# A hand-ordered attention and gating block: tile 0 in halves, first queries by token halves, new orders

## The chip, the core and the metric

The kernel runs on one core of a Trainium2 chip. The metric is the device time of one execution, in microseconds. The engines are named as in the profile: PE (TensorE), DVE (VectorE), ACT (ScalarE), POOL (GpSimd) and SP (SyncE, which only issues DMAs here). PEld is PE's loading of weights.

## What is computed

```python
h  = x + A(layernorm(x), wqkv, wo)
h2 = h + B(layernorm(h), w_in, w_sp, b_sp, w_out)

# A: linear attention, 32 heads of 16
q, k, v = split(x @ wqkv)
phi = lambda t: where(t > 0, t + 1, exp(t)) + 1e-6
kv, z = einsum(phi(k), v), sum(phi(k))
o = (phi(q) @ kv) / (phi(q) . z + 1e-6)
A = o @ wo

# B: gated mixing
z  = gelu(x @ w_in);  z1, z2 = first half, layernorm(second half)
g  = w_sp @ z2 + b_sp          # mixes tokens
B  = (z1 * g) @ w_out
```

x has 2048 tokens of 512, all data are bf16; w_in has 1792 columns, w_sp is 2048 x 2048.

## The kernel before

The 2048 tokens are 16 tiles of 128, and four groups of four tiles. The stages are these.

1. Tile n of x is loaded (`load`, L495), its statistics are made on DVE (L576, L580), the factor from the variance on ACT for tiles 0 to 3 (L590 Ln, L592 Exp) and on POOL for the pairs above (L595, L597), and DVE normalises it into `xn1` (L611, in the profile pk_xn_z). It is transposed into `xT`: tiles 0 to 3 on PE (L645), with a copy out of PSUM on ACT (L652); the others by a DMA transpose that SP issues (L637).
2. Keys of a pair of tiles (`kv_proj`, L734) and queries of a group (`q_proj`, L748) come out of PSUM through `phi`: an exp on ACT (L711), for most also a relu on ACT (L713), then on DVE a small step (L714) and a sum (L717), or, where there is no relu, one longer step that reads PSUM (L720). `pk`, the result for keys, goes into a product with xn1 that is summed over all tiles (L766); the values are applied to that sum later.
3. Denominators (`den`) come for two groups at a time: a product with PE (L858), Ln and Exp on ACT (L863, L866), a spread over partitions on PE (L874), copies on ACT (L880), and a multiplication of the queries on DVE (L887). The attention output is L909 on PE, its residual sum L914 on DVE.
4. The second normalisation of a tile runs over DVE (statistics, L576 and L580 again), POOL (L626, L595, L597, L627) and ACT (L618, into the four buffers of `xn`), and SP transposes the tile into `hT` by DMA (L637). Then PE makes the second half of w_in's product tile by tile (L944, seven eighths of two banks), ACT its gelu (L949), DVE its statistics (L953); and the first half, the gate, in groups of four tiles (L975, gelu L980).
5. The mixing matmuls (L1014), the bias and the gating on DVE (L1021, L1023), the output projection (L1032) with the residual (L1038), and the stores (L1040) fill the second half of the run.

The weights and biases wv, wo, w_in, the spatial bias (`bsp`, 512 KB into e) and w_out are loaded by DMAs that stand in POOL's row of instructions; SP's row holds the loads of x, of the queries' weights, the transposes of tiles and those of the spatial weights (`wsp`, L990).

The order of all this is no loop's: the code records about 790 operations with what they read and write, and `ORDER`, a list of their numbers, says in which order they go to the five engines' rows. `SLOT` gives each PSUM or buffer tile its place. Each row runs strictly in order. Waits on semaphores are worked out from the data and from the reuse of places. Ahead of the real work PE runs matmuls on constants (`keep_busy`, L564), eight at once and then some behind named operations:

```python
for gate, n, cost, count in ((first[0], 512, MM, 2), (rs_op[0], 512, MM, 1), (tr_op[0], 256, MM / 2, 2),
                             (tr_op[1], 256, MM / 2, 2)):
```

Of the kernel before, what the change touches and what calls it, by code (L numbers as in the profile page):

```python
# [10 lines left out]
P = 128  # L11
# [38 lines left out]
]  # L50
SLOT = [
# [303 lines left out]
def bass_sequential_preLN__linear_attn_block__mixer_gmlp__prompt_kernel(  # L355
# [26 lines left out]
    CENTRED = ()  # L382
    A_STATS = ()
# [91 lines left out]
    def bank(i):  # L475
        return lambda a: a[:, i, :]
# [13 lines left out]
    def dve_c(n, mode=1):  # L490
        return 0.08 + 0.00103 * n / mode
# [124 lines left out]

    def normalise_act(dst, src, rs, nm, n=512):
        op("act", act_c(n, 2) + 0.04, lambda e: e.activation(dst.ap(), src.ap(), ACT.Identity, bias=nm.ap(), scale=rs.ap()),  # L618
           r=[src, rs, nm], w=[dst])
# [11 lines left out]
    def transposed(n, src, dst, by_pe, bias=0.0):  # L631
# [8 lines left out]
        t = Tile(PS)  # L640

        def tr(e):
            o = t(as_bf).ap()
            for c in range(KD):
                i = e.transpose(o[:, c * P:(c + 1) * P], src().ap()[:, c * P:(c + 1) * P], ident.all().ap())  # L645
            return i
        tr_op[n] = op("pe", 4 * MS, tr, r=[src(), ident.all()], w=[t()], bias=bias, after=warm)
        if n in COPY_DVE and dst is not hT:
            op("dve", dve_c(512), lambda e: e.tensor_copy(
                d.ap(), t(as_bf).ap()[:, 0:D].rearrange("p (c t) -> p c t", c=KD)), r=[t()], w=[d], bias=bias)  # L650
            return
        op("act", act_c(512), lambda e: e.activation(  # L652
            d.ap(), t(as_bf).ap()[:, 0:D].rearrange("p (c t) -> p c t", c=KD), ACT.Copy), r=[t()], w=[d], bias=bias)


    last_lnexp = []
    first = {}
    rs_of, rs_op = {}, {}
# [433 lines left out]
```

## Time and profile before

| | |
|---|---|
| median of 3 runs | 240.75 us (240.72 to 240.87) |
| the profiled execution | 240.84 us, its span 239.6 us |
| PE busy | 234.9 us, 98% |
| DVE busy | 132.0 us, 55% |
| ACT busy | 79.0 us, 33% |
| POOL busy | 35.7 us, 15% |
| granted PE clock | 1.0 |

In the profile a row of the timeline gives start and duration in us from the span's start, the engine, the line of the kernel, the operation, its output and inputs, and in brackets the idle time before it with what ended it. A matmul's duration includes its way through the array, so two that follow each other overlap in the records: one of 512 columns is listed with 379 ns, and the next one starts 216 ns after it. The chain of waits gives only the time that each step adds.

### The profile page before, as it was taken

The numbers are of one execution on the slowest core, as the hardware profiler recorded it, in microseconds if no ns is written. First come the engines' busy times: TensorE is split into PE (matmuls) and PEld (weight loads), VectorE is DVE, ScalarE is ACT, GpSimd is POOL, SyncE is SP. The second block draws the span as 40 slices with busy tenths as digits, with TensorE's granted clock in tenths as the row PEclk, the third lists the DMA queues.
The fourth block names the chain that finished last, engine by engine and source line by source line (L and its number), as shares of the span: only waits on it lengthen the run. The fifth ranks groups of instructions, "written<-read, shape, count | busy, mean of one in ns | idle before, by whom it ended". The sixth has DMA issues, their size and how long they took to land.

```text
span 239.6 us, 3005 instructions
## 1 busy us (share of the span) xinstructions
PE 234.9 (98%) x1163; PEld 109.3 (46%) x1186; DVE 132.0 (55%) x269; ACT 79.0 (33%) x101; POOL 35.7 (15%) x84
## 2 busy tenths in 40 slices
PE   8999999999999999999999999999999999999996
PEld 2544444454444445544444444444444444444443
DVE  4899774399999843989233233341333513323444
ACT  3894744784368889656301000000000000000000
POOL 7113403000626310058100000000000000000000
PEclk9999999999999999999999999999999999999999
DMA  7941439970146442448944434444100200000022
GB/s 213 311 82 33 87 78 248 319 147 0 24 90 152 89 90 44 108 93 83 239 94 109 92 88 102 96 109 113 43 0 0 67 23 0 0 0 3 0 87 88
DMA packets 56702, 21.83 MB, mean 91 GB/s; under 512 B 50704, under 2 KB 55824, under 8 KB 56688
## 3 DMA queue, kind: packets, MB, share of 16 engines
q1 hardware_dynamic: 54928, 16.62, 31.1%
q0 software_dynamic: 944, 4.33, 6.8%
q10 hardware_dynamic: 816, 0.70, 0.9%
q8 instruction: 9, 0.15, 0.3%
q14 instruction: 5, 0.04, 0.1%
HBM read 7.47 MB, written 2.10 MB: 40 GB/s over the span
## 4 chain that ended last, share of the span: by engine, by line
PE 95%; DVE 1%; DMA 1%; issue 1%; ACT 0%
PE ps L1014 40%; PE ps L944 10%; PE ps L1032 10%; PE ps L975 10%; PE ps L748 6%; PE ps L734 6%; PE ps L766 6%; PE ps L909 5%; DMA xh<-in_A_x_dram 1%; DVE small L576 1%; PE ps L858 0%; PE ps L838 0%; PE ps L782 0%; PE ps L819 0%; PE ps L645 0%
## 5 line engine op out<-in xcount | busy, mean ns | idle before, releaser
L1014 PE MATMUL ps<-wsp,pk_xn_z 128*128 128x512 bf16 x330 | 72.9, 379 | 0.3
L1021 DVE TENSOR_TENSOR e<-ps,e 128x512 bf16<-128x512 f32 x28 | 19.3, 691 | 68.3 <-PE ps L1014 68.3
L1014 PEld LDWEIGHTS ps<-wsp,pk_xn_z 128*128 128x128 bf16 x336 | 32.9, 98 | 39.7
L944 PE MATMUL ps<-win,hT 128*128 128x512 bf16 (+1 forms) x127 | 25.5, 352 | 0.1
L975 PE MATMUL ps<-hT,win 128*128 128x512 bf16 x108 | 25.3, 379 | 0.2
L1032 PE MATMUL ps<-wout,xT_pq_z 128*128 128x512 bf16 (+2 forms) x117 | 24.6, 366 | 0.1
L1014 PE MATMUL ps<-wqkv_wsp,pk_xn_z 128*128 128x512 bf16 x109 | 24.2, 379 | 0.2
L953 DVE BATCH_NORM_STATS2 small<-pk_xn_z 128x6 f32<-128x512 bf16 (+1 forms) x32 | 18.4, 609 | 8.8 <-ACT pk_xn_z L949 8.7
L576 DVE BATCH_NORM_STATS2 small<-xh 128x6 f32<-128x512 bf16 x32 | 20.7, 673 | 3.9 <-DMA xh<-in_A_x_dram 3.9
L711 ACT ACTIVATE e<-ps 128x1024 bf16<-128x1024 f32 x16 | 16.4, 1026 | 11.3 <-PE ps L734 9.5
L980 ACT ACTIVATE xT_pq_z<-ps 128x1024 bf16<-128x1024 f32 (+1 forms) x16 | 14.3, 916 | 16.0 <-PE ps L975 16.0
L944 PEld LDWEIGHTS ps<-win,hT 128*128 128x128 bf16 x128 | 12.5, 98 | 12.4
L1032 PEld LDWEIGHTS ps<-wout,xT_pq_z 128*128 128x128 bf16 x119 | 11.5, 98 | 13.0
L1038 DVE TENSOR_TENSOR e<-ps,xh 128x512 bf16<-128x512 f32 (+2 forms) x17 | 11.2, 660 | 11.3 <-PE ps L1032 11.3
L1014 PEld LDWEIGHTS ps<-wqkv_wsp,pk_xn_z 128*128 128x128 bf16 x112 | 11.0, 98 | 13.2
L975 PEld LDWEIGHTS ps<-hT,win 128*128 128x128 bf16 x112 | 11.0, 98 | 12.5
L597 POOL TENSOR_TENSOR small<-small 128x2 f32<-128x2 f32 x22 | 16.3, 747 | 1.3
L949 ACT ACTIVATE pk_xn_z<-ps 128x896 bf16<-128x896 f32 x16 | 14.2, 916 | 6.4 <-PE ps L944 6.4
L766 PE MATMUL ps<-pk_xn_z 128*128 128x512 bf16 x63 | 15.9, 379 | 0.2 <-issue 0.2
L734 PE MATMUL ps<-wqkv_wsp,xT_pq_z 128*128 128x512 bf16 x63 | 15.7, 379 | 0.1
L748 PE MATMUL ps<-xT_pq_z,wqkv_wsp 128*128 128x512 bf16 x61 | 14.9, 380 | 0.2
L909 PE MATMUL ps<-pk_xn_z,xT_pq_z 128*128 128x512 bf16 x62 | 14.2, 379 | 0.1
(71 smaller groups left out, 172.9 us busy)
## 6 DMA issues: line engine op xcount, KB each, us to landing
out_dram<-e SPq DMA_DIRECT2D x15, 128.0 KB, 1.7
win<-in_B_w_in_dram POOLq DMA_DIRECT2D x1, 1792.0 KB, 11.3
xh<-in_A_x_dram SPq DMA_DIRECT2D x4, 256.0 KB, 6.8
wout<-in_B_w_out_dram POOLq DMA_DIRECT2D x1, 896.0 KB, 9.3
wsp<-in_B_w_sp_dram SPq DMA_TRANSPOSE x48, 2.7
wqkv_wsp<-in_A_wqkv_dram ACTq DMA_DIRECT2D x1, 512.0 KB, 4.3
wqkv_wsp<-in_A_wqkv_dram SPq DMA_DIRECT2D x1, 512.0 KB, 6.2
xh<-in_A_x_dram SPq DMA_DIRECT2D x1, 512.0 KB, 8.0
```

The lines of the kernel that those rows point to most:

```text
L576: op("dve", dve_c(512), lambda e: e.bn_stats(s6.ap(), src.ap()), r=[src], w=[s6])
L711: op("act", act_c(n), lambda e: e.activation(lo.ap(), t(flat).ap(), ACT.Exp), r=[t()], w=[lo])
L734: i = e.matmul(t(bank(ti)).ap(), lhsT=lhs.ap()[:, c, :], rhs=rhs.ap()[:, c, :], start=(c == 0), stop=(c == KD - 1))
L748: r_ = e.matmul(t(bank(i)).ap(), lhsT=lhs.ap()[:, c, :], rhs=rhs.ap()[:, c, :], start=(c == 0), stop=(c == KD - 1))
L766: r = e.matmul(txk[h](bank(i)).ap(), lhsT=xx.ap()[:, c * P:(c + 1) * P], rhs=kk.ap(), start=(n == 0), stop=(n == NT - 1))
L909: i = e.matmul(t(bank(ti)).ap(), lhsT=l.ap()[:, c, :], rhs=mw[c, :].ap(), start=(c == 0), stop=(c == KD - 1))
L944: k = e.matmul(t(bank(i)).ap()[:, 0:b - a], lhsT=l.ap()[:, c, :], rhs=win[c, a:b].ap(), start=(c == 0), stop=(c == KD - 1))
L953: op("dve", dve_c(b - a), lambda e, s6=s6, src=src: e.bn_stats(s6.ap(), src.ap()), r=[src], w=[s6])
L975: k = e.matmul(t(bank(i)).ap(), lhsT=l.ap()[:, c, :], rhs=r_.ap()[:, c, :], start=(c == 0), stop=(c == KD - 1))
L1014: k = e.matmul(t(bank(0)).ap(), lhsT=l.ap()[:, s - a, :], rhs=r_.ap()[:, s - a, :], start=(s == 0), stop=(s == NT - 1))
L1021: op("dve", dve_c(512), lambda e: e.tensor_tensor(gb().ap(), t(bank(0)).ap(), bsp().ap()[:, tg * GW:(tg + 1) * GW], ALU.add), r=[t(), bsp( ...
L1032: k = e.matmul(t(bank(0)).ap()[:, 0:b - a], lhsT=l.ap()[:, fc, :], rhs=wout[fc, a:b].ap(), start=(fc == 0), stop=(fc == KF - 1))
```

## The change

The copy of tile 0's transposes goes out of PSUM in two column halves, each an ACT instruction of 256 columns, and tile 0's keys are made in two steps of two matmuls, each of which needs one half. The queries of the first group are made in two token halves: a matmul has 256 columns instead of 512, and each half needs only tiles 0 and 1, or 2 and 3. The two fillers behind tile 1's transposes are dropped. The lists ORDER and SLOT are new throughout. What is computed stays the same. Lines of the kernel move down by up to 24: L734, L748, L766, L858, L874, L909, L944, L949, L975 become L751, L769, L790, L882, L898, L933, L968, L973, L999; L564, L645, L652, L618 and L637 become L565, L651, L661, L623 and L642.

The core of the diff (branches of constants that this kernel leaves empty are cut):

```diff
 ORDER = [
-    1, 18, 13, 19, 2, 26, 0, 35, 36, 3, 4, 5, 6, 7, 27, 28, 14, 37, 38, 29, 30, 8, 9, 10, 17, 20, 24, 42, 43, 44, 45,
+    13, 18, 21, 17, 14, 24, 27, 0, 3, 4, 5, 1, 2, 26, 35, 36, 37, 28, 29, 30, 31, 32, 6, 11, 38, 15, 7, 12, 19, 16, 33,
...
+    N_HALVES, T_HALVES, Q_HALVES = (), (0,), (0,)
...
-        t = Tile(PS)
-
-        def tr(e):
-            o = t(as_bf).ap()
-            for c in range(KD):
-                i = e.transpose(o[:, c * P:(c + 1) * P], src().ap()[:, c * P:(c + 1) * P], ident.all().ap())
-            return i
-        tr_op[n] = op("pe", 4 * MS, tr, r=[src(), ident.all()], w=[t()], bias=bias, after=warm)
...
-        op("act", act_c(512), lambda e: e.activation(
-            d.ap(), t(as_bf).ap()[:, 0:D].rearrange("p (c t) -> p c t", c=KD), ACT.Copy), r=[t()], w=[d], bias=bias)
+        whole, halves = ((0, KD),), ((0, KD // 2), (KD // 2, KD))
+        for a, b in halves if n in N_HALVES else whole:
+            t = Tile(PS)
...
+            for u, v in halves if n in T_HALVES and n not in N_HALVES else ((a, b),):
+                to = dst[n // TPG][u:v, (n % TPG) * P:(n % TPG + 1) * P]
+                copy = lambda e, t=t, u=u, v=v, to=to: e.activation(
+                    to.ap(), t(as_bf).ap()[:, u * P:v * P].rearrange("p (c t) -> p c t", c=v - u), ACT.Copy)
...
+                op("act", act_c(P * (v - u)), copy_rest if u else copy, r=[t()], w=[to], bias=bias)
...
-    for gate, n, cost, count in ((first[0], 512, MM, 2), (rs_op[0], 512, MM, 1), (tr_op[0], 256, MM / 2, 2),
-                                 (tr_op[1], 256, MM / 2, 2)):
+    for gate, n, cost, count in ((first[0], 512, MM, 2), (rs_op[0], 512, MM, 1), (tr_op[0], 256, MM / 2, 2)):
...
+            for a, b in ((0, KD // 2), (KD // 2, KD)) if n in T_HALVES else ((0, KD),):
+                lhs = xT[n // TPG][a:b, (n % TPG) * P:(n % TPG + 1) * P]
+                rhs = wqkv[a:b, col:col + D]
...
     def q_proj(gq, f):
         t = Tile(PS, 2)
-        for i in range(2):
-            lhs = wqkv[:, f + i:D:KD]
-            rhs = xT[gq].all()
...
+        for a, b in ((0, GW // 2), (GW // 2, GW)) if gq in Q_HALVES else ((0, GW),):
+            for i in range(2):
+                lhs = wqkv[:, f + i:D:KD]
+                rhs = xT[gq][:, a:b]
```

The order on PE at the start, before. L564 are fillers, L645 a tile's transposes, L734 keys, L748 queries, L766 the sum of pk with xn1:

```order
L564 MATMUL ps<-const-bfloat16-1.0 128x512 x11
L645 MATMUL ps<-small,pk_xn_z 128x128 x4
L564 MATMUL ps<-const-bfloat16-1.0 128x256 x2
L645 MATMUL ps<-small,pk_xn_z 128x128 x4
L564 MATMUL ps<-const-bfloat16-1.0 128x256
L734 MATMUL ps<-wqkv_wsp,xT_pq_z 128x512 x4
L645 MATMUL ps<-small,pk_xn_z 128x128 x4
L734 MATMUL ps<-wqkv_wsp,xT_pq_z 128x512 x4
L645 MATMUL ps<-small,pk_xn_z 128x128 x4
L564 MATMUL ps<-const-bfloat16-1.0 128x256
L734 MATMUL ps<-wqkv_wsp,xT_pq_z 128x512 x8
L748 MATMUL ps<-xT_pq_z,wqkv_wsp 128x512 x16
```

and after the change (L651 transposes, L751 keys, L769 queries):

```order
L651 MATMUL ps<-small,pk_xn_z 128x128 x4
L565 MATMUL ps<-const-bfloat16-1.0 128x256 x2
L651 MATMUL ps<-small,pk_xn_z 128x128 x4
L751 MATMUL ps<-wqkv_wsp,xT_pq_z 128x512 x8
L651 MATMUL ps<-small,pk_xn_z 128x128 x4
L769 MATMUL ps<-xT_pq_z,wqkv_wsp 128x256 x4
L651 MATMUL ps<-small,pk_xn_z 128x128 x4
L769 MATMUL ps<-xT_pq_z,wqkv_wsp 128x256 x4
L751 MATMUL ps<-wqkv_wsp,xT_pq_z 128x512 x4
L769 MATMUL ps<-xT_pq_z,wqkv_wsp 128x256 x4
L751 MATMUL ps<-wqkv_wsp,xT_pq_z 128x512 x4
L769 MATMUL ps<-xT_pq_z,wqkv_wsp 128x256 x20
```

Keys of tiles 0 and 1 run one after the other, and queries stand between the last transposes and the keys of tiles 2 and 3.

PE around the last denominators, before (L909 the attention output, L858 the denominators' product, L874 their spread, L944 the second half of w_in):

```order
L909 MATMUL ps<-pk_xn_z,xT_pq_z 128x512 x20
L858 MATMUL ps<-xT_pq_z,small 32x256 x16
L909 MATMUL ps<-pk_xn_z,xT_pq_z 128x512 x4
L874 MATMUL ps<-wsp 128x256 x4
L909 MATMUL ps<-pk_xn_z,xT_pq_z 128x512 x40
```

and after:

```order
L933 MATMUL ps<-pk_xn_z,xT_pq_z 128x512 x16
L882 MATMUL ps<-xT_pq_z,small 32x256 x16
L933 MATMUL ps<-pk_xn_z,xT_pq_z 128x512 x8
L898 MATMUL ps<-wsp 128x256 x4
L933 MATMUL ps<-pk_xn_z,xT_pq_z 128x512 x32
```

The product comes four matmuls earlier, and eight instead of four lie between it and the spread.

POOL around the load of the spatial bias, before (L627 and L632 are the last small product of a pair's second normalisation, L595 and L596 the first step of a factor):

```order
L627 TENSOR_TENSOR small<-small 128x2 [waits s_pool]
L626 TENSOR_SCALAR small<-small 128x2
L597 TENSOR_TENSOR small<-small 128x2 [waits s_pool]
L627 TENSOR_TENSOR small<-small 128x2 [waits s_pool]
L495 DMA e<-in_B_b_sp_dram 128x2048
```

and after:

```order
L632 TENSOR_TENSOR small<-small 128x2 [waits s_pool]
L631 TENSOR_SCALAR small<-small 128x2
L596 TENSOR_SCALAR small<-small 128x2 [waits s_dve] x2
L632 TENSOR_TENSOR small<-small 128x2 [waits s_pool]
L496 DMA e<-in_B_b_sp_dram 128x2048
```

Before, the load stood behind the small products of tiles 0 to 7. Now it stands behind those of all sixteen tiles and behind the first steps of two factors of the gelu's output; the second of these waits for an aggregate on DVE that is queued behind the statistics of tile 8's gelu.

PE behind tile 8, after the change (d_ThT9 is the landing of tile 9's transpose in hT; L968 a tile's second half of w_in, L999 the gate):

```order
L968 MATMUL ps<-win,hT 128x512 [waits d_ThT9,s_act]
L968 MATMUL ps<-win,hT 128x512 x3
L968 MATMUL ps<-win,hT 128x384 x4
L968 MATMUL ps<-win,hT 128x512 [waits d_ThT11,s_act]
L968 MATMUL ps<-win,hT 128x512 x3
L968 MATMUL ps<-win,hT 128x384 x4
L968 MATMUL ps<-win,hT 128x512 [waits d_ThT10,s_act]
L968 MATMUL ps<-win,hT 128x512 x3
L968 MATMUL ps<-win,hT 128x384 x4
L999 MATMUL ps<-hT,win 128x512 [waits s_act]
L999 MATMUL ps<-hT,win 128x512 x3
L968 MATMUL ps<-win,hT 128x512 [waits d_ThT13,s_act]
```

and ACT there (L973 gelu, first of tile 8 and then of tile 6; L623 the normalisation of tile 13, whose transpose SP issues next):

```order
L1004 ACTIVATE xT_pq_z<-ps 128x1024 [waits s_pe]
L973 ACTIVATE pk_xn_z<-ps 128x896 [waits s_pe]
L973 ACTIVATE pk_xn_z<-ps 128x896
L623 ACTIVATE xn<-xh,small 128x512 [waits d_ThT9]
L973 ACTIVATE pk_xn_z<-ps 128x896 [waits s_pe] x2
```

Tiles 9, 11 and 10 and four gate matmuls stand on PE between tile 8 and tile 13.

More of the change, by code (lines that the diff above doesn't have):

```diff
@@ L639, in transposed, with tr, tr_rest, copy_rest @@
             return
-        t = Tile(PS)
-        def tr(e):
-            o = t(as_bf).ap()
-            for c in range(KD):
-                i = e.transpose(o[:, c * P:(c + 1) * P], src().ap()[:, c * P:(c + 1) * P], ident.all().ap())
-            return i
-        tr_op[n] = op("pe", 4 * MS, tr, r=[src(), ident.all()], w=[t()], bias=bias, after=warm)
[L648 to L652, printed above, removed]
-            d.ap(), t(as_bf).ap()[:, 0:D].rearrange("p (c t) -> p c t", c=KD), ACT.Copy), r=[t()], w=[d], bias=bias)
+        whole, halves = ((0, KD),), ((0, KD // 2), (KD // 2, KD))
+        for a, b in halves if n in N_HALVES else whole:
+            t = Tile(PS)
+            def tr(e, t=t, a=a, b=b):
+                for c in range(a, b):
+                    i = e.transpose(t(as_bf).ap()[:, c * P:(c + 1) * P], src().ap()[:, c * P:(c + 1) * P],
+                                    ident.all().ap())
+                return i
+            def tr_rest(e, tr=tr):
+                return tr(e)
+            tr_op[n] = op("pe", (b - a) * MS, tr_rest if a else tr, r=[xn1[n, a * P:b * P], ident.all()], w=[t()],
+                          bias=bias, after=warm)
+            for u, v in halves if n in T_HALVES and n not in N_HALVES else ((a, b),):
+                to = dst[n // TPG][u:v, (n % TPG) * P:(n % TPG + 1) * P]
+                copy = lambda e, t=t, u=u, v=v, to=to: e.activation(
+                    to.ap(), t(as_bf).ap()[:, u * P:v * P].rearrange("p (c t) -> p c t", c=v - u), ACT.Copy)
+                def copy_rest(e, copy=copy):
+                    return copy(e)
+                op("act", act_c(P * (v - u)), copy_rest if u else copy, r=[t()], w=[to], bias=bias)
     last_lnexp = []
@@ L728, in kv_proj, with mm, rest @@
             n = 2 * p + ti
[L729 to L737 removed]
+            for a, b in ((0, KD // 2), (KD // 2, KD)) if n in T_HALVES else ((0, KD),):
+                lhs = xT[n // TPG][a:b, (n % TPG) * P:(n % TPG + 1) * P]
+                rhs = wqkv[a:b, col:col + D]
+                def mm(e, ti=ti, lhs=lhs, rhs=rhs, a=a, b=b):
+                    for c in range(a, b):
+                        i = e.matmul(t(bank(ti)).ap(), lhsT=lhs.ap()[:, c - a, :], rhs=rhs.ap()[:, c - a, :],
+                                     start=(c == 0), stop=(c == KD - 1))
+                    return i
+                def rest(e, mm=mm):
+                    return mm(e)
+                k_pe.append(op("pe", (b - a) * MM, rest if a else mm, r=[lhs, rhs], w=[t()]))
         return t
@@ L741, in q_proj, with mm, rest @@
         t = Tile(PS, 2)
-        for i in range(2):
-            lhs = wqkv[:, f + i:D:KD]
-            rhs = xT[gq].all()
-            def mm(e, i=i, lhs=lhs):
-                for c in range(KD):
-                    r_ = e.matmul(t(bank(i)).ap(), lhsT=lhs.ap()[:, c, :], rhs=rhs.ap()[:, c, :], start=(c == 0),
-                                  stop=(c == KD - 1))
-                return r_
-            op("pe", 4 * MM, mm, r=[lhs, rhs], w=[t()])
+        for a, b in ((0, GW // 2), (GW // 2, GW)) if gq in Q_HALVES else ((0, GW),):
+            for i in range(2):
+                lhs = wqkv[:, f + i:D:KD]
+                rhs = xT[gq][:, a:b]
+                def mm(e, i=i, lhs=lhs, rhs=rhs, a=a, b=b):
+                    for c in range(KD):
+                        r_ = e.matmul(t(bank(i)).ap()[:, a:b], lhsT=lhs.ap()[:, c, :], rhs=rhs.ap()[:, c, :],
+                                      start=(c == 0), stop=(c == KD - 1), skip_group_check=True)
+                    return r_
+                def rest(e, mm=mm):
+                    return mm(e)
+                op("pe", 4 * MM * (b - a) / GW, rest if a else mm, r=[lhs, rhs], w=[t()])
         phi(t, pqT[gq][f:f + 2, :], relu=Q_RELU[gq])
```

17 lines of the change are left out of this document (8 added, 9 removed), and 72 rows, old and new, of tables (ORDER, SLOT).

## The prediction

> **What bounds the kernel now.** The page comes first: the span, and how busy each engine is. Then PE alone by stretches (columns: stretch, its length, then PE, PEld, DVE, ACT and POOL busy, granted clock, DMA share and GB/s).
>
> ```profile
> span 239.6 us, 3005 instructions
> PE 234.9 (98%) x1163; PEld 109.3 (46%) x1186; DVE 132.0 (55%) x269; ACT 79.0 (33%) x101; POOL 35.7 (15%) x84
> ...
> 6.50:57.00 50.50, 50.10 (x291) 24.15 (x297) 38.65 (x82) 33.92 (x43) 9.26 (x15) 1.00 0.61 151
> 57.00:60.00 3.00, 2.80 (x29) 1.08 (x28) 3.00 (x5) 1.20 (x3) 0.00 (x0) 1.00 0.00 0
> 60.00:237.00 177.00, 176.10 (x822) 82.00 (x838) 86.51 (x175) 41.26 (x51) 21.66 (x50) 1.00 0.32 70
> ```
>
> PE is the bound, at full clock, from 6.5 us to the end, and the matmuls after the change take the same time: sixteen of 512 columns become thirty-two of 256. So only three things can move the end: how early PE starts its real work, fillers that stand in its row, and waits in it. Any new wait of PE is lost for good. The profiled run took 240.84 us, its span 239.6; the median of the runs is 240.75, 0.09 less. The sum is made against 240.84.
>
> Next the timeline at the start, and one piece of the chain (start, duration, what).
>
> ```profile
> 5.50 0.20 ACT L592 ACTIVATE small<-small 128x1 f32<-128x1 f32 x1
> 6.08 0.39 DVE L611 TENSOR_SCALAR pk_xn_z<-xh,small 128x512 bf16<-128x512 bf16 x1
> 6.13 0.60 ACT L652 ACTIVATE xT_pq_z<-ps 128x512 bf16<-128x512 bf16 x1 [0.42 <-PE ps L645]
> 6.76 0.27 PE L564 MATMUL ps<-const-bfloat16-1.0 128*128 128x256 bf16 x1
> 6.87 1.03 PE L734 MATMUL ps<-wqkv_wsp,xT_pq_z 128*128 128x512 bf16 x4
> 9.15 1.89 PE L734 MATMUL ps<-wqkv_wsp,xT_pq_z 128*128 128x512 bf16 x8
> 14.33 1.03 PE L766 MATMUL ps<-pk_xn_z 128*128 128x512 bf16 x4
> 15.20 2.00 PE L734 MATMUL ps<-wqkv_wsp,xT_pq_z 128*128 128x512 bf16 x8
> ...
> 9.21 0.11 PE ps L564
> ```
>
> The copy of tile 0's transposes ends at 6.73, and the first keys start 0.14 later, at 6.87: that copy sets the start. A filler of 0.11 stands at 9.2. Eight key matmuls take 1.89 at 9.15 but 2.00 at 15.20: there PE waited 0.11 for a transpose (tile 5).
>
> **The start.** Two copies of 256 columns stand where one of 512 was.
>
> ```profile
> L711 ACT ACTIVATE e<-ps 128x1024 bf16<-128x1024 f32 x16 | 16.4, 1026 | 11.3 <-PE ps L734 9.5 <-PE ps L748 1.3 <-DVE e L714 0.5
> ```
>
> 1024 columns take 1.03, 512 take 0.60, so 256 take 0.60 - 0.43/2 = 0.39; the other end is 0.48, a 128x256 pass of another function (L863, quoted below). I take 0.39, since it is the same kind of pass. Then the first half is there at 6.52 and the keys start at 6.66, 0.21 earlier (0.12 with the other price). Tile 1's transposes, in front of them on PE, don't hold them: its normalisation no longer stands behind tile 2's statistics, starts right after the exp that ends at 5.70 and ends at 6.17 instead of 6.47. The second half copy ends by 6.8, its keys come at 7.09; tile 1's copy ends about 7.3, its keys come at 7.52, with 0.08 to spare. The filler before tile 3's keys is gone: 0.11. The first queries are now wanted at about 8.6 instead of 10.9.
>
> ```profile
> 2.17 0.43 SPq L495 DMA_DIRECT2D wqkv_wsp<-in_A_wqkv_dram  x1
> wqkv_wsp<-in_A_wqkv_dram SPq DMA_DIRECT2D x1, 512.0 KB, 6.2
> ```
>
> Their weights land at 2.17 + 6.2 = 8.4: 0.2 of cover, and beyond that each 0.1 of lateness costs 0.1. So PE reaches the first L790 (L766 before) at 14.33 - 0.21 - 0.11 = 14.01. But that matmul needs pk of tiles 0 and 1:
>
> ```profile
> 11.85 0.74 DVE L611 TENSOR_SCALAR pk_xn_z<-xh,small 128x512 bf16<-128x512 bf16 x2
> 12.50 0.42 DVE L714 TENSOR_SCALAR e<-e 128x1024 bf16<-128x1024 bf16 x1
> 12.99 1.19 DVE L720 SCALAR_TENSOR_TENSOR pk_xn_z<-ps,e 128x1024 bf16<-128x1024 f32 x1
> ```
>
> pk was there at 14.18 and PE began at 14.33: no slack even before. On DVE the work ahead of it is bound by the loads of x, which don't move; one small aggregate fewer stands between, so pk comes at about 14.08 and PE starts at 14.23. **Of 0.32 gained, 0.22 is lost to this wait; 0.10 stays** (0 to 0.32).
>
> **Tile 5's wait.** Ten L790 instead of four now run ahead of the keys of tiles 4 and 5, 6 x 0.216 = 1.3 later, while tile 5's normalisation is 0.3 later: the wait goes, **-0.11**. A new small one comes at 21: the next queries need the PSUM that the third pk releases. From the last key matmul that is 0.17 drain + 1.03 exp + 0.42 + 1.19 and four handovers (0.3) = 3.1, with 14 matmuls, 3.02, beside it: **+0.07** (0 to 0.15).
>
> **The last denominators.** The chain of waits, and the timeline of both spreads:
>
> ```profile
> 58.28 0.48 ACT wsp L863
> 58.77 0.02 issue
> 58.79 0.42 ACT wsp L866
> 59.22 0.14 issue
> 59.35 0.29 PE ps L874 x4
> ...
> 45.67 1.03 PE L748 MATMUL ps<-xT_pq_z,wqkv_wsp 128*128 128x512 bf16 x4
> 46.63 0.29 PE L874 MATMUL ps<-wsp 32*128 32x256 bf16 x4
> ...
> 58.16 1.04 PE L909 MATMUL ps<-pk_xn_z,xT_pq_z 128*128 128x512 bf16 x4
> ```
>
> Four matmuls issue in 4 x 0.216 = 0.86. At 45.67 the spread follows 0.10 after them; at 58.16 it follows 0.33 after, so 0.23 is waiting for Ln and Exp (0.48 + 0.42). Now eight matmuls, 1.73, lie between, and the residual additions on DVE stand behind the queries: **-0.23** (-0.23 to 0). Without anything else the sum is 240.84 - 0.10 - 0.11 + 0.07 - 0.23 = 240.47.
>
> **The new order of the middle.** Here lies the term that decides. POOL issues the load of the spatial bias (bsp, 512 KB). Rows of the transposes of hT and of that load, each with its time from issue to landing (min/median/max); first four transposes with no load beside them, then the one issued right behind the load, then the load:
>
> ```profile
> L637 SPq DMA_TRANSPOSE hT<-xn x4: 1188/1240/1267, 64.1 to 68.1; - x4
> ...
> DMA to landing us min/median/max: 2.4/2.5/2.5
> ...
> L637 SPq DMA_TRANSPOSE hT<-xn x1: 1201/1201/1201, 73.1 to 73.1; - x1
> ...
> DMA to landing us min/median/max: 4.6/4.6/4.6
> ...
> L495 POOL DMA_DIRECT2D e<-in_B_b_sp_dram x1: 648/648/648, 73.0 to 73.0; - x1
> ...
> DMA to landing us min/median/max: 4.0/4.0/4.0
> ```
>
> A transpose beside the load lands at 77.7, 0.6 after the load, and takes 4.6 instead of 2.5. Before, that cost nothing: tiles 4 to 6 were transposed there, well ahead of their matmuls. Now the load stands later on POOL, behind the sums of tiles 14 and 15, and I count from the start G of tile 8's gelu on ACT (L973):
>
> ```profile
> 84.45 1.72 ACT L949 ACTIVATE pk_xn_z<-ps 128x896 bf16<-128x896 f32 x2
> 63.22 1.52 ACT L618 ACTIVATE xn<-xh,small 128x512 bf16<-128x512 bf16 x2 [2.45 <-POOL small L627]
> L953 DVE BATCH_NORM_STATS2 small<-pk_xn_z 128x6 f32<-128x512 bf16 x16 | 10.8, 683 | 8.8 <-ACT pk_xn_z L949 8.7
> 73.77 0.22 POOL L595 TENSOR_SCALAR small<-small 128x2 f32<-128x2 f32 x1
> 80.48 4.54 PE ps L944 x24
> 99.93 0.86 PE ps L975 x4
> ```
>
> On ACT two gelus start 0.80 apart, and tile 13's normalisation (0.80 long) follows them: it ends at G + 2.4, its transpose issues at G + 2.46. On POOL: gelu 0.92, statistics of DVE 0.68, an aggregate 0.1 longer, the sum on POOL 0.22, one small product 0.2: the load issues at about G + 2.2, 0.25 before the transpose. So the pair stands as at 73.0, and the transpose lands between G + 2.2 + 4.0 + 0.6 = G + 6.8 and G + 2.46 + 4.6 = G + 7.06. PE, from the end of tile 8 (0.2 before G), has tiles 9, 11 and 10 at 4.54/3 = 1.51 each and four gate matmuls, 0.86: it wants tile 13 at G + 5.2. An undisturbed transpose would land at G + 4.96, just in time; this one makes PE wait 6.85 - 5.2 = 1.65 to 7.1 - 5.2 = 1.9. I take **+1.8**. PE's row is fixed, so the gate matmuls behind tile 13 can't fill it, and nothing after it gives it back.
>
> The Trainium skill, "DMA: Bandwidth & Descriptors", section "Queues, rings and completion order", states that each DMA engine takes turns between the queue rows that have work, one packet at a time. Read as turns of about equal bytes, that rule gives the second rival below, 241.3; the row at 73.1 speaks against this reading, since the transpose landed only behind the whole load.
>
> The load of w_out moves by a little too; its first use lies behind all gate matmuls and hundreds of mixing matmuls, so it costs nothing.
>
> **The sum.** 240.84 - 0.37 + 1.80 = 242.27; less 0.09 for the median, **242.2**. A measurement of this kernel can tell about 0.2% (0.48 us) from no change.
>
> **The rivals.**
> - *Not slower: load and transpose miss each other.* For it: an undisturbed transpose would be in time, by 0.2, and the place of each was counted from durations, not seen. Against: both hang on the same gelu, so what shifts one shifts the other. It decides where the load issues after most of the transpose's 2.5 us are over, or so early that it lands before G + 4.6. Then only -0.37 is left: 240.4. Chance 0.17, mostly within 0.2%; all of the pk wait would have to go too for over 0.2% faster.
> - *Shared evenly.* If the transpose gives way only to as many bytes as it has, 128 of 512 KB, it is delayed by 4.0/4 = 1.0, lands at G + 2.46 + 3.5 = G + 5.96, and PE waits 0.8: 241.3. For it: only three transposes are seen beside this load, and none alone. Against: the one issued right behind it took 4.6. Chance 0.11.
> - *More waits beside it.* PE stands on waits of under 0.2 at the query weights (8.4 against 8.6), at tile 1's keys (0.08) and at pk; with 0.2 to 0.6 more: 242.5 to 242.9. Against: the order before had covers as thin, and of 50.5 us from 6.5 to 57 PE sat idle in 0.4, of 177 after 60 in 0.9. Chance 0.08.
>
> **How the numbers follow.** The forecast has 0.64, at 241.8 to 242.6: wait 1.65 to 1.9, start 0 to 0.32, denominators 0 to 0.23. The range reaches down through the shared case into the upper half of the first rival, and up to part of the last: 240.5 to 242.7, which leaves out about 0.15. Faster by over 0.2% (under 240.27): 0.05, from the first rival. Within 0.2%: 0.14, the rest of it and a little of the second. Slower: 0.81.
>
> **What would show it.** In the profile after, PE idle of 1.6 to 1.9 us at about 94 to 97, released by the DMA of hT from xn; the load of e issued a quarter of a microsecond before a transpose that takes over 4 us to land; no idle PE at the last spread; first keys at about 6.66; PE waiting about 0.2 for pk near 14. If that transpose lands in 2.5, the forecast is wrong and the first rival holds. If PE idles at the hT transposes of other tiles, my covers there were wrong.

## The result, and the profile after

| | before | after |
|---|---|---|
| median | 240.81 us (240.72 to 240.88, 6 runs) | 242.28 us (242.06 to 242.81, 6 runs) |
| ratio | 1 | 1.0065 (95%: 1.0052 to 1.0078) |
| profiled execution, its span | 240.84, 239.6 | 242.06, 240.8 |

The changed kernel is slower by 1.5 us. Run once more beside the kernel before, it took 242.11 against 240.88, ratio 1.0055 (1.0034 to 1.0075).

The page after, and PE by the same stretches as before (stretch, length, then PE, PEld, DVE, ACT, POOL busy, granted clock, DMA share, GB/s):

```profile
span 240.8 us, 3059 instructions
PE 235.8 (98%) x1200; PEld 110.4 (46%) x1200; DVE 132.5 (55%) x269; ACT 78.9 (33%) x102; POOL 34.7 (14%) x84
...
6.50:57.00 50.50, 50.48 (x322) 25.27 (x320) 39.43 (x83) 34.24 (x44) 9.09 (x15) 1.00 0.62 149
57.00:60.00 3.00, 3.00 (x18) 1.26 (x17) 2.91 (x7) 2.94 (x5) 0.22 (x1) 1.00 0.03 5
60.00:237.00 177.00, 175.24 (x829) 80.81 (x828) 85.85 (x172) 38.84 (x49) 20.64 (x50) 1.00 0.32 70
```

Up to 60 us PE now stands still less than before (busy 50.48 of 50.50 and 3.00 of 3.00). The loss lies behind 60: 1.76 us idle there. The page's groups give it to one place, and the timeline and one piece of the chain show how it comes about:

```profile
L968 PE MATMUL ps<-win,hT 128*128 128x512 bf16 (+1 forms) x128 | 25.7, 352 | 1.8 <-DMA hT<-xn 1.8
...
89.08 1.73 ACT L973 ACTIVATE pk_xn_z<-ps 128x896 bf16<-128x896 f32 x2 [0.78 <-PE ps L968]
90.69 0.81 ACT L623 ACTIVATE xn<-xh,small 128x512 bf16<-128x512 bf16 x1
91.22 0.65 POOL L496 DMA_DIRECT2D e<-in_B_b_sp_dram  x1
93.42 1.03 PE L999 MATMUL ps<-hT,win 128*128 128x512 bf16 x4
96.21 2.54 PE L968 MATMUL ps<-win,hT 128*128 128x512 bf16 x12 [1.76 <-DMA hT<-xn]
...
91.53 4.55 DMA hT<-xn
...
L496 POOL DMA_DIRECT2D e<-in_B_b_sp_dram x1: 648/648/648, 91.2 to 91.2; - x1
...
DMA to landing us min/median/max: 4.2/4.2/4.2
```

On ACT come two gelus and a normalisation. The load of the spatial bias issues at 91.22, and 0.31 later, at 91.53, the transpose of tile 13, which takes 4.55 us. The load took 4.2, so the transpose lands 0.64 behind it. PE's last matmul ahead began at 94.07; the next could have begun at 94.28 and begins at 96.21: 1.93 us lost (the 1.76 in brackets counts from the end of that matmul's way through the array).

The start of after, then of a second profile of before (start, duration, engine, line):

```profile
5.49 0.38 PE L651 MATMUL ps<-small,pk_xn_z 128*128 128x128 bf16 x4 [0.17 <-DVE pk_xn_z L612]
6.35 1.90 PE L751 MATMUL ps<-wqkv_wsp,xT_pq_z 128*128 128x512 bf16 x8
12.23 1.22 DVE L736 SCALAR_TENSOR_TENSOR pk_xn_z<-ps,e 128x1024 bf16<-128x1024 f32 x1
13.76 2.32 PE L790 MATMUL ps<-pk_xn_z 128*128 128x512 bf16 x10
```

```profile
5.72 0.38 PE L645 MATMUL ps<-small,pk_xn_z 128*128 128x128 bf16 x4 [0.19 <-DVE pk_xn_z L611]
6.88 1.03 PE L734 MATMUL ps<-wqkv_wsp,xT_pq_z 128*128 128x512 bf16 x4
12.40 1.19 DVE L720 SCALAR_TENSOR_TENSOR pk_xn_z<-ps,e 128x1024 bf16<-128x1024 f32 x1
14.34 1.03 PE L766 MATMUL ps<-pk_xn_z 128*128 128x512 bf16 x4
```

From tile 0's transposes to the first keys it is 0.86 now and was 1.16. The first L790 starts 0.58 earlier; 0.23 of that is that tile 0's transposes themselves came earlier (5.49 against 5.72), which a second profile of after doesn't show (5.76). Last, the stage of the last denominators:

```profile
56.24 0.62 PE L882 MATMUL ps<-xT_pq_z,small 128*32 128x256 bf16 x16
58.62 0.29 PE L898 MATMUL ps<-wsp 32*128 32x256 bf16 x4
...
57.85 1.28 ACT L958 ACT_TABLE_LOAD   x1
```

From product to spread it is 2.38, with eight matmuls (1.73) between: 0.65 besides. Before it was 59.35 - 57.61 = 1.74 with four (0.86): 0.88. So 0.23 of waiting is gone. The load of the gelu's table, which ran at 67.56 before, has moved into this place on ACT; I hadn't seen that.

The matmul work is the same in both kernels, but for 0.05 us at the start (below). So a profile can be read as a sum: the start of a landmark less the work that stands ahead of it on PE (7.80 us ahead of the first L766 or L790, for instance) is PE's idle time up to there, the fillers counted as idle. The landings are those of the keys' weights.

| us | before | before, again | after | after, again | load early | load and aggregate early |
|---|---|---|---|---|---|---|
| keys' weights landed | 5.55 | 5.58 | 5.66 | 5.58 | 5.49 | 5.42 |
| tile 0's transposes, first keys | 5.71, 6.87 | 5.72, 6.88 | 5.49, 6.35 | 5.76, 6.62 | 5.76, 6.62 | 5.75, 6.82 |
| idle up to the first L766 / L790 | 6.54 | 6.55 | 5.96 | 6.23 | 6.23 | 6.42 |
| up to the first L782 / L806 | 6.75 | 6.64 | 6.24 | 6.33 | 6.76 | 6.58 |
| product to spread, less the matmuls between | 0.88 | 0.88 | 0.65 | 0.66 | 0.65 | 0.66 |
| lost ahead of tile 13 | 0 | 0 | 1.93 | 1.70 | 0 | 0 |
| idle in the whole span | 10.49 | 10.39 | 11.69 | 11.56 | 10.28 | 10.11 |

The two second profiles: -0.32 (start), +0.01 (up to L806), -0.22 (denominators), +1.70 (tile 13), together +1.17, which is their whole difference.

### The profile page after: what moved, and what is told of

Read it like the earlier page. It is cut to its first block, busy times and chain, and to the rows that moved or that the text cites. A ratio compares the mean times of both kernels' runs of the same rounds, so it can differ in the third digit from the quotient of the medians.

```text
span 240.8 us, 3059 instructions
## 1 busy us (share of the span) xinstructions
PE 235.8 (98%) x1200; PEld 110.4 (46%) x1200; DVE 132.5 (55%) x269; ACT 78.9 (33%) x102; POOL 34.7 (14%) x84
## 3 DMA queue, kind: packets, MB, share of 16 engines
q1 hardware_dynamic: 54928, 16.62, 31.9%
q0 software_dynamic: 944, 4.33, 6.0%
## 4 chain that ended last, share of the span: by engine, by line
PE 94%; DMA 3%; ACT 1%; DVE 1%; issue 0%
PE ps L1038 40%; PE ps L1056 10%; PE ps L999 10%; PE ps L968 8%; PE ps L769 6%; PE ps L790 6%; PE ps L933 6%; PE ps L751 6%; DMA hT<-xn 2%; DMA xh<-in_A_x_dram 1%; ACT pk_xn_z L973 1%; DVE small L577 1%; PE ps L651 1%; PE ps L882 0%; PE ps L862 0%; PE ps L806 0%
## 5 line engine op out<-in xcount | busy, mean ns | idle before, releaser
L968 PE MATMUL ps<-win,hT 128*128 128x512 bf16 (+1 forms) x128 | 25.7, 352 | 1.8 <-DMA hT<-xn 1.8
L999 PE MATMUL ps<-hT,win 128*128 128x512 bf16 x112 | 25.6, 379 | 0.0
L968 PEld LDWEIGHTS ps<-win,hT 128*128 128x128 bf16 x128 | 12.4, 98 | 14.4 <-ACT pk_xn_z L973 2.2
L999 PEld LDWEIGHTS ps<-hT,win 128*128 128x128 bf16 x112 | 11.0, 98 | 12.6
L598 POOL TENSOR_TENSOR small<-small 128x2 f32<-128x2 f32 x22 | 16.2, 742 | 1.0
L790 PE MATMUL ps<-pk_xn_z 128*128 128x512 bf16 x64 | 16.2, 379 | 0.0
L973 ACT ACTIVATE pk_xn_z<-ps 128x896 bf16<-128x896 f32 x16 | 14.2, 915 | 5.8 <-PE ps L968 5.8
L596 POOL TENSOR_SCALAR small<-small 128x2 f32<-128x2 f32 x22 | 6.8, 309 | 64.5 <-DVE small L581 64.2
L769 PE MATMUL ps<-xT_pq_z,wqkv_wsp 128*128 128x512 bf16 (+1 forms) x80 | 15.9, 337 | 0.0
L751 PE MATMUL ps<-wqkv_wsp,xT_pq_z 128*128 128x512 bf16 x64 | 15.6, 379 | 0.0
```

The lines of the kernel that those rows point to most:

```text
L751: i = e.matmul(t(bank(ti)).ap(), lhsT=lhs.ap()[:, c - a, :], rhs=rhs.ap()[:, c - a, :], start=(c == 0), stop=(c == KD - 1))
L769: r_ = e.matmul(t(bank(i)).ap()[:, a:b], lhsT=lhs.ap()[:, c, :], rhs=rhs.ap()[:, c, :], start=(c == 0), stop=(c == KD - 1), skip_group_che ...
L790: r = e.matmul(txk[h](bank(i)).ap(), lhsT=xx.ap()[:, c * P:(c + 1) * P], rhs=kk.ap(), start=(n == 0), stop=(n == NT - 1))
L968: k = e.matmul(t(bank(i)).ap()[:, 0:b - a], lhsT=l.ap()[:, c, :], rhs=win[c, a:b].ap(), start=(c == 0), stop=(c == KD - 1))
L973: gelus.append(op("act", act_c(FH), lambda e, t=t, d=d: e.activation(d.ap(), t(flat).ap()[:, 0:FH], ACT.Gelu_apprx_tanh), r=[t()], w=[d], ...
L999: k = e.matmul(t(bank(i)).ap(), lhsT=l.ap()[:, c, :], rhs=r_.ap()[:, c, :], start=(c == 0), stop=(c == KD - 1))
```

## The experiments

Numbers in ORDER: 603 is the load of the spatial bias, 300 the first small step of a second normalisation on POOL, 516 and 517 tile 13 on PE.

**The load out of the way.**

```diff
-    ..., 299, 297, 300, 302, ...    458, 408, 603, 485, ...
+    ..., 299, 297, 603, 300, 302, ...    458, 408, 485, ...
```

> The changed kernel with one thing moved: the load of the spatial bias (L496, into e) stands on POOL ahead of the first small product of the second normalisations, so that it issues near 57 us and lands near 61, before the first transpose into hT at 62.8. Theory (the wait of 1.76 to 1.93 us before tile 13 is made by that load beside that transpose): the transpose of tile 13 lands in about 2.5 us, PE has no wait there, and the time is 242.28 - 1.8 = 240.5 (240.2 to 240.7); the scatter of the runs (0.75 between lowest and highest) goes too if the load makes it. Rival A (the transpose of tile 13 is late for another reason, the weights' transposes around it or the buffers of xn): it still takes over 4 us, and the time stays at 242.3. Rival B (the wait goes but another place of PE waits instead, for example at tiles 14 and 15): 241 to 242.

240.57 us (240.06 to 241.4) against 240.88, ratio 0.999 (0.9978 to 1.0003). The load issues at 56.83 and lands at 61.15. Tile 13's transpose, and the only wait of PE for a transpose that is left:

```profile
L642 SPq DMA_TRANSPOSE hT<-xn x1: 1190/1190/1190, 92.0 to 92.0; - x1
...
DMA to landing us min/median/max: 2.4/2.4/2.4
...
20.49 1.04 PE L751 MATMUL ps<-wqkv_wsp,xT_pq_z 128*128 128x512 bf16 x4 [0.25 <-DMA xT_pq_z<-pk_xn_z]
```

The load makes the wait: without it the transpose takes 2.4, PE doesn't stop, and 1.5 to 1.7 us come back. It doesn't make the scatter: this kernel scatters as before does on that chip (240.44 to 241.74). A wait of 0.42 for tile 7's transpose at 20 eats the whole gain of the start (6.76 idle up to L806, before 6.64 to 6.75); it is taken up below.

**One step later.** 603 stands behind 427 (one small product, L598) on POOL.

> The changed kernel with the load of the spatial bias one instruction later on POOL, behind the small product L598 (0.73 us) that followed it: it issues about 0.5 us behind the transpose of tile 13 instead of 0.31 us ahead of it. Theory as predicted (the transpose is held behind the whole load only because the load is first): it lands in 2.5 to 3.2, PE waits 0.1 to 0.8, time 240.5 to 241.2. Rival (which is first doesn't matter, the load's traffic holds the transpose up whenever the two overlap, and the transpose lands 0.6 behind the load): the load lands at 96.3, the transpose near 96.9, PE waits 2.7, time 243.1.

241.82 us, ratio 1.003 (1.002 to 1.004). The transpose of tile 13, then PE:

```profile
L642 SPq DMA_TRANSPOSE hT<-xn x1: 1190/1190/1190, 92.1 to 92.1; - x1
...
DMA to landing us min/median/max: 3.8/3.8/3.8
...
96.02 1.19 PE L968 MATMUL ps<-win,hT 128*128 128x512 bf16 x5 [0.97 <-DMA hT<-xn]
```

Neither text was right. The load issued 0.37 behind the transpose and landed at 97.04; the transpose landed at 95.88, 1.16 ahead of it, but 1.3 later than undisturbed, and PE lost 1.13. Being first is worth something, not everything; which part of the transpose came late is shown below, with the second rival.

**Three steps later.** 603 stands behind 443.

> The changed kernel with the load of the spatial bias three instructions later on POOL: it issues about 1.4 to 1.8 us behind the transpose of tile 13 and 2 ahead of tile 14's. Theory as corrected by the run with the load one step later (what counts is how much of the load's traffic falls into the 2.5 us of the transpose): the transpose of tile 13 lands in 2.5 to 2.8, PE waits 0 to 0.3; tiles 14 and 15 have over 1 us to spare; time 240.5 to 240.9. Rival (the load, once issued, holds up tile 14 and 15 by 2 each, and their cover is thinner than I think): a wait of 0.3 to 1 at tile 14, 241 to 241.6.

240.55 us, ratio 0.9984 (0.9969 to 0.9999). Tile 13's transpose took 2.4 with the load 1.36 behind it; tile 14's took 3.1, and PE waited for neither. So the loss ends somewhere between 0.4 and 1.4 us of distance behind the transpose: 1.7 us of shift against it, which cost nothing, undo it.

**Half of the load.**

```diff
-            load("pool", "bsp", bsp(), B_b_sp.partition_broadcast(P), ...)
+            for a, b in ((0, S // 2), (S // 2, S)):
+                load("pool", "bsp", bsp(lambda v, a=a, b=b: v[:, a:b]), B_b_sp[a:b].partition_broadcast(P), ...)
```

> The changed kernel with the load of the spatial bias in two halves of 256 KB: the first early on POOL, as in the run with the whole load early, the second at the place that the whole load has in the changed kernel. Theory (the transpose lands behind the whole load, so what it loses goes with the bytes of the load): of 2.1 us lost by the transpose (4.55 against 2.45) half is left, 1.0, the transpose lands near G + 2.45 + 3.5 and PE waits 0.7 to 0.9; time 241.2 to 241.5. Rival (even sharing, the transpose gives way to about its own 128 KB, whatever the size of the load as long as that is larger): the delay stays 2.1 and the time 242.3. Second rival (a fixed price of a load issued just ahead): the same, 242.3.

242.1 us, ratio 1.0042 (1.0026 to 1.0058). The transpose, then the half that stands ahead of it:

```profile
DMA to landing us min/median/max: 4.0/4.0/4.0
...
L496 POOL DMA_DIRECT2D e<-in_B_b_sp_dram x1: 639/639/639, 91.9 to 91.9; - x1
...
DMA to landing us min/median/max: 3.6/3.6/3.6
```

The transpose again landed 0.67 behind the load, so "behind the whole load" holds. What fell is my price: half of the bytes took only 0.6 off the load's 4.2, so PE still lost 1.35, between the texts (0.8, and 1.8 and over). By its time the run is nearer to the rivals' 242.3, but the profiled run, 242.17, had the keys' weights at 7.02, so part of that is the start.

**PE's row filled.** Ops 568, 570 and 571 (twelve gate matmuls) stand ahead of 516, and the gelu 496 ahead of the normalisations 411 and 409.

> The changed kernel with its load where it is, but PE's row changed: twelve gate matmuls (L999, of tiles 8 to 11) that stood behind tile 13 stand ahead of it, 12 x 0.216 = 2.6 us, and on ACT the gelu that frees the PSUM of eight of them stands ahead of two normalisations instead of behind. Theory (PE lost time only because its fixed row had nothing ready ahead of tile 13): the transpose still takes 4.5 us and lands near 96.1, PE reaches tile 13 at 94.2 + 2.6 = 96.8 and doesn't wait; time 240.4 to 240.8. Rival (the matmuls moved are then missing behind, at tiles 14 and 15 whose normalisations come 0.9 later): a wait of 0.3 to 1 there, time 240.8 to 241.5.

240.84 us, ratio 0.9996 (0.9985 to 1.0007). Tile 13's transpose, then PE:

```profile
DMA to landing us min/median/max: 4.3/4.3/4.3
...
94.04 3.62 PE L999 MATMUL ps<-hT,win 128*128 128x512 bf16 x16
97.49 2.70 PE L968 MATMUL ps<-win,hT 128*128 128x512 bf16 x12
```

The transpose is as late as ever (4.3), and PE, busy with sixteen gate matmuls, doesn't notice. No wait follows at tiles 14 and 15. The time is just above the 240.4 to 240.8 of the theory. In this profile the keys' weights landed at 6.90 and the keys began at 7.03, so nothing of the start's gain is in it.

**The collision put into the kernel before.** The load 599 behind 422 on POOL, made to wait for tile 13's normalisation:

```diff
-            load("pool", "bsp", bsp(), ..., bias=-120.0, cost=1.0)
+            load("pool", "bsp", bsp(), ..., bias=-120.0, cost=1.0, behind=[g.ops[392]])
```

> The kernel before with one thing moved: the load of the spatial bias stands behind the first step of a factor of tiles 8 and 9 on POOL and waits there for the normalisation of tile 13 on ACT, so that it issues within 0.1 us of tile 13's transpose, near 91.9, as it did with tile 4's at 73.04. Theory (load beside a transpose that PE soon needs): that transpose takes 4.5 instead of 2.5 us and lands near 96.5; PE wants tile 13 at 95.0 and waits 1.4 to 1.6; time 240.86 + 1.5 = 242.2 to 242.5. Rival (it needs the changed order around it, other transposes and normalisations, to become a wait): 240.7 to 241.0.

241.3 us, ratio 1.0013 (1.0002 to 1.0024): +0.42. The transposes of tiles 12 and 13, the load, and PE:

```profile
L637 SPq DMA_TRANSPOSE hT<-xn x2: 1216/1245/1274, 90.4 to 91.7; - x2
...
DMA to landing us min/median/max: 3.5/3.9/4.3
...
90.00 0.65 POOL L495 DMA_DIRECT2D e<-in_B_b_sp_dram  x1 [2.43 <-ACT xn L618]
95.23 3.20 PE L944 MATMUL ps<-win,hT 128*128 128x512 bf16 x16 [0.28 <-DMA hT<-xn]
```

I had misread ACT's row: tile 13 is normalised there ahead of tile 12, so the load issued at 90.0, 0.43 ahead of tile 12's transpose (4.3 us) and 1.69 ahead of tile 13's (3.5). That one is late by 1.0, PE had 0.6 of cover and lost 0.44, start to start. So neither text had the time. The size is another than expected, the mechanism the same (tile 12's transpose lands 0.67 behind the load, as tile 13's does in the changed kernel), and it needs nothing of the changed order.

**The wait at 20.** On DVE the aggregate of tile 7's statistics (77) goes back in front of the keys' long pass (134), as it stood before the change; the load is early too.

```diff
-    70, 133, 71, 141, 72, 218, 219, 220, 134, ..., 77, 143, ...
+    70, 133, 71, 141, 72, 218, 219, 220, 77, 134, ..., 143, ...
```

> The run with the load early, and one more move: on DVE the aggregate of tile 7's statistics (L581, 0.17 us) stands ahead of the long pass that makes the keys of tiles 0 and 1 (L736, 1.22 us), as it did before the change, instead of behind it. New theory (the start's gain was lost because that aggregate releases the factor of tiles 6 and 7 on POOL, and with it their normalisation and transposes, which PE then waits for by 0.42 at 20): the transposes of tiles 6 and 7 issue about 1 us earlier, the wait at 20 goes, the idle time of PE up to the first product for the values (L806) falls from 6.76 to 6.3 to 6.5, and the time from 240.57 to 240.2 (240.0 to 240.4). Rival (the step as I predicted it: the keys' pass is what PE waits for near 14, and with the aggregate in front it comes 0.1 later): a wait of 0.1 at the first L790 and no gain, 240.6 to 240.7.

240.38 us (239.89 to 240.58), ratio 0.9977 (0.9969 to 0.9986): faster than both kernels. With the load early alone, and then with the aggregate in front:

```profile
12.67 1.22 DVE L736 SCALAR_TENSOR_TENSOR pk_xn_z<-ps,e 128x1024 bf16<-128x1024 f32 x1
13.80 0.17 DVE L581 BATCH_NORM_AGGREGATE small<-small 128x2 f32<-128x6 f32 x1
14.06 0.46 POOL L596 TENSOR_SCALAR small<-small 128x2 f32<-128x2 f32 x1 [2.42 <-DVE small L581]
15.78 0.74 DVE L612 TENSOR_SCALAR pk_xn_z<-xh,small 128x512 bf16<-128x512 bf16 x2 [0.61 <-POOL small L598]
```

```profile
12.63 0.17 DVE L581 BATCH_NORM_AGGREGATE small<-small 128x2 f32<-128x6 f32 x1
12.89 0.22 POOL L596 TENSOR_SCALAR small<-small 128x2 f32<-128x2 f32 x1 [1.28 <-DVE small L581]
15.28 0.73 DVE L612 TENSOR_SCALAR pk_xn_z<-xh,small 128x512 bf16<-128x512 bf16 x2
```

The factor starts 1.2 earlier on POOL, the normalisation of tiles 6 and 7 only 0.5 earlier, since DVE now has other steps in front of it. The idle time between the first L790 and the first L806 falls from 0.53 to 0.16. The time fell by 0.19 where I expected 0.37: in this profile the start itself was 0.19 worse (keys at 6.82). The 0.19 between the two medians is not clear of the scatter of the runs (240.06 to 241.4 against 239.89 to 240.58); that the run beats the kernel before is.

**The halves, one by one,** both from the kernel just shown: T_HALVES = () and Q_HALVES = ().

> The run before it (load early, aggregate early) with tile 0's copy out of PSUM whole again, one ACT instruction of 512 columns, and tile 0's keys in one step. Theory (the copy sets the start of the keys): the keys start 0.2 later behind tile 0's transposes, and nothing later takes it up now that the wait at 20 is gone: 0.15 to 0.25 more than the run before it. Rival (the keys' weights set the start: they landed between 5.5 and 7.0 in the profiles so far, and the keys began 0.13 behind a landing at 7.0): where they land after 6.5 the halves bring nothing, 0 to 0.1.

> The run with load and aggregate early, with the first group's queries whole again, 512 columns to a matmul and both token halves at once, at the place of the second halves. Theory (the halves stand where PE waits for the copies of tiles 2 and 3, about 0.9 us of matmuls between the last transposes and the keys of tile 2): without them PE idles 0.3 to 0.9 there, 240.5 to 241.1. Rival (there is slack, since the keys of tiles 0 and 1 that stand in front are long enough): 0 to 0.2 more than with the halves.

With the whole copy 240.57 us, ratio 0.9988 (0.9977 to 0.9998): 0.19 more, which is not clear of the scatter either. With whole queries 240.94, ratio 1.0007 (0.9997 to 1.0017): 0.56 more. The starts, whole copy first, then whole queries:

```profile
5.75 0.38 PE L651 MATMUL ps<-small,pk_xn_z 128*128 128x128 bf16 x4 [0.20 <-DVE pk_xn_z L612]
6.83 1.90 PE L751 MATMUL ps<-wqkv_wsp,xT_pq_z 128*128 128x512 bf16 x8
...
6.62 1.90 PE L751 MATMUL ps<-wqkv_wsp,xT_pq_z 128*128 128x512 bf16 x8
8.35 0.83 PE L651 MATMUL ps<-small,pk_xn_z 128*128 128x128 bf16 x8
9.43 1.04 PE L751 MATMUL ps<-wqkv_wsp,xT_pq_z 128*128 128x512 bf16 x4 [0.25 <-ACT xT_pq_z L661]
```

From the same 5.75 the keys start at 6.83 with the whole copy and at 6.62 with the halves: 0.21. The profiles as wholes don't show this gain: PE idles 10.06 with the whole copy and 10.11 in the kernel that both runs start from, whose keys began at 6.82 in its profile. The queries' halves fill the time in which tile 3's normalisation and the copies of tiles 2 and 3 run; without them PE stops twice, by 0.21 and 0.41.

**The denominators back.** With the load early, the product 283 stands one step (four matmuls) later on PE.

> The run with the load early (without the aggregate's move), with the product of the last denominators four matmuls later on PE, as before the change: four instead of eight matmuls lie between it and the spread; DVE's order stays. Theory (the spread waited for Ln and Exp, 0.23 before): a wait of 0.2 ahead of the last spread comes back, the idle time between that product and the spread rises from 0.22 to 0.42 to 0.45, time 0.2 more than the run with the load early. Rival (what helped was the order on DVE, the residual sums behind the queries): no wait, 0.

241.35 us, ratio 1.0017 (1.0007 to 1.0027), 0.78 more than with the load early alone. ACT behind Exp, and PE behind the spread:

```profile
59.66 1.28 ACT L958 ACT_TABLE_LOAD   x1
60.95 1.08 ACT L904 ACTIVATE wsp<-ps 128x512 bf16<-128x512 f32 x2
...
62.33 1.04 PE L933 MATMUL ps<-pk_xn_z,xT_pq_z 128*128 128x512 bf16 x4 [0.42 <-DVE xT_pq_z L911]
```

The wait ahead of the spread is back (the spread begins 0.32 behind the issue of the last matmul, 0.10 otherwise), 0.22 as expected. Behind it comes one that I had not foreseen: the table's load, 1.28 us, now stands between Exp and the copies of the spread, the copies begin at 60.95, and PE waits another 0.59, start to start. So the earlier product also pays for the table's load in its new place.

**Both kernels again.**

> The kernel before, unchanged, for a second profile of it, to see how far its start moves by itself. In the first the keys' weights landed at 5.55, the keys began at 6.87, PE had idled 6.54 up to the first L766 and 6.75 up to the first product for the values (L782). Theory (the weights' landing moves the start in both kernels, the keys beginning no earlier than 0.13 behind it): with a landing below 6.7 the same numbers within 0.1; with 7.0, about 0.3 more. Rival (the changed order made the start more sensitive): below 0.1 whatever the landing.

> The changed kernel, unchanged, on this chip and in a second profile. Theory: the wait ahead of tile 13 is again 1.7 to 2.0, the transpose lands 0.55 to 0.7 behind the load, and the time is 1.3 to 1.7 over the kernel before; the start differs with the landing of the keys' weights. Rival (the wait in the first profile was an unlucky one): a wait under 1.5.

Before: 240.75 us. The loads of x landed 0.6 earlier than in the first profile (8.56 against 9.17 for tiles 4 and 5), pk was there 0.6 earlier (13.59), and PE still began L766 at 14.34. After: 242.11, wait 1.70, landing 0.64 behind the load; the first profile was no accident. The time is 1.23 over the kernel before, a little under the 1.3 to 1.7 of the theory. In five profiles with the keys' weights at 6.43 or later (6.43 to 7.35) the keys began 0.13 or 0.14 behind their landing, in one of them with the order of before.

## Why the prediction was right

**PE is the bound; only its start, fillers and waits count.** It held: the difference between the two second profiles is found as idle PE to 0.01.

**The collision, +1.8.** 1.93 and 1.70, at the place named, 94 to 96. Counted from the start of tile 8's gelu, 89.08: load issued at +2.14 (said 2.2), transpose at +2.45 (2.46), landed at +7.00 (6.8 to 7.06). It is shown from four sides: the load away, the load later, PE filled, and the collision made in the other kernel. Where the two missed each other, the time came close to the first rival's 240.4: 240.57 and 240.55.

**Even sharing (the second rival).** It gave 0.8 of waiting and fell for a load that is ahead. The Trainium skill, "DMA: Bandwidth & Descriptors", section "Queues, rings and completion order", has the queues take turns packet by packet; read with turns of equal bytes it gave this rival. The profile's count of packets speaks for turns of unequal bytes:

```profile
q1 hardware_dynamic: 54928, 16.62, 31.9%
q0 software_dynamic: 944, 4.33, 6.0%
```

A packet of SP's queue has 16.62 MB / 54928 = 0.3 KB, one of POOL's 4.33 MB / 944 = 4.6 KB, fifteen times as much. With turns of one such packet each the load would pass almost alone, with a few of the transpose's packets between its own.

The single packets in the traces show this at one distance only. The load is 128 packets of 4 KB, a transpose 512 of 256 bytes; at the end of each come closing packets of 4 bytes. Before, at tile 4, with the load 0.05 ahead at issue, the two alternate: from the first packet of a transpose at 74.89 to the load's first closing packet at 76.12, 97 of each start. After, with the load 0.31 ahead, they don't. The load's packets start from 92.57 on; the transpose's first starts at 94.27, 2.75 behind its issue instead of 1.17 with the load away, right behind the load's first closing packet. The four other profiles with the load 0.30 to 0.43 ahead (the second of after, the half load, PE's row filled, the collision in the kernel before) show the same. With the load 0.37 behind, all packets of the transpose have started by 94.06, before the load's first at 94.17; only its closing packets come late, the last at 95.53 instead of 94.13 with the load away.

So the one that is clearly first passes whole, and the turns of the rule show only where the two arrive together. Why this is so stays open: a packet of that rule need not be one packet of the profile, and the size of the packets was not varied.

**The start, -0.10 kept of 0.32.** The gain was sized right as a total, 0.32 in the two second profiles, and its main part too: 0.21 for the halves of the copy (6.83 against 6.62). The rest came otherwise than I said, and that it adds up is luck. Tile 0's transposes come 0.04 later (5.76 against 5.72). The keys begin 1.16 behind them before and 0.86 after, 0.30 less; of this, the 0.09 besides the copy is mostly the other filler that was dropped, which stood on PE ahead of the keys until 6.87 (with the whole copy and without that filler the keys begin 1.08 behind). From the keys to the first L790 only 0.05 is gained, not the filler's 0.11, for a matmul of 256 columns takes 0.109 and one of 512 takes 0.216: thirty-two for sixteen cost 0.05, which I had put at nothing. The step that failed is the wait for pk, which was to take 0.22 of it. It never came. I had taken the 0.15 between pk and the first L766 of one profile for a bound; it was chance, from loads of x that were late in that run.

**Tile 5, -0.11, and the wait at 21, +0.07.** The first was there in one of two profiles of before, so it was no fixed price. The second did not show. What showed is a wait for tiles 6 and 7 at 19 to 20 of 0 to 0.5. I had counted the aggregate that moved behind pk as a gain of 0.1 for pk, and not asked who waits for it: POOL's factor, the normalisation, two transposes, PE.

**The last denominators, -0.23.** -0.22 to -0.23 in every profile. The step left out the table's load that moved there; it was covered.

**The sum.** For the start with its small waits it had -0.14. The two first profiles differ there by -0.51, the two second ones by -0.31, and with the load early the gain was 0; so a term that I gave one number moves by half a microsecond from run to run. The sum of 242.27 was for a profiled run, and the profiled runs took 242.06 and 241.94, 0.2 to 0.3 less. That the median came out at 242.28, so close to the forecast's 242.2, is in part luck. **More waits (the third rival)** came, at tiles 6 and 7, but no larger than what the start gave.

## What to carry to other kernels

When an order moves a large load, look for the small transfers issued in the next half microsecond, and for the engine whose next instruction needs one: ask how far apart they must be, since half the size helped little, and 1.4 us of distance behind the transpose helped wholly. A slack read from one profile is no bound where it ends in a transfer; take a second profile of the same kernel first. For each small instruction that an order moves behind a long one, follow its result to the end, on the other engines too.

## What was unexpected of the hardware

- What a transpose of 128 KB loses to a load of 512 KB depends on their distance at issue: load 0.31 ahead, 4.3 to 4.55 us; 0.05 ahead, 4.58 (before, tile 4); 0.37 behind, 3.75; 1.36 behind or away, 2.41.
- A load of 256 KB takes 3.6 us where one of 512 KB takes 4.0 to 4.2 in the same place; near 57 us the other half took 3.9 and whole loads 3.9 to 4.3.
- The keys' weights land between 5.4 and 7.35 us from one profile to the next, the load of tiles 4 and 5 between 8.55 and 9.6. Most of the runs' scatter can come from there; that it does was not tried.
- In three of fourteen profiles some or all of PE's first four transposes came at half their speed, 0.107 apart instead of 0.055, with the same fillers ahead and at a granted clock of 1.00. In the kernel with the denominators back all four did, in 0.63 instead of 0.38 us; the row of the timeline and the stretch around it:

```profile
5.48 0.63 PE L651 MATMUL ps<-small,pk_xn_z 128*128 128x128 bf16 x4
...
5.40:6.40 1.00, 1.00 (x10) 0.91 (x10) 0.80 (x2) 0.42 (x2) 0.18 (x1) 1.00 0.85 226
```

The Trainium skill, "TensorE: Matmul & The Clock Gate", section "Part 1: The HAM clock gate (the "warmup" mystery)", says that PE is released from half rate only after a busy window that runs freely, so that the moment differs from run to run, and gives 107 and 56 ns for such a pair. The spacings here agree with that; the granted clock of the row does not show it, and no run tried the cause.

- Some transposes take 3.3 to 4.1 us with no load beside them, at the same place in each profile of a kernel (before, at 82.6: 4.1 twice). That cause is open too.
